# The second long convolution in the first one's step order, and the last slice's two halves in PSUM tiles of their own

## The chip, the cores and the metric

The kernel runs on one core of one Trainium2 chip. The metric is the device time of one execution in microseconds (us); lower is better. Engines are named as the profile names them: PE is TensorE (PEld its weight loads), DVE is VectorE, ACT is ScalarE, POOL is GpSimd, SP is the engine whose queue issues most DMAs. PSUM is the memory that PE writes its results to; DVE and ACT copy them from there to SBUF.

## The reference

Two layers, each a long convolution (an S4 state-space model) and a local dilated attention, each behind a layer norm and added to the running `x` (2048 tokens, 512 channels, bfloat16):

```python
def _A_ref(u, ...):                       # long convolution, per channel d
    P = jnp.exp(logdA[:, :, None] * l[None, None, :])
    K = jnp.einsum("dn,dnl,dn->dl", Cc, P, dB).real
    ...
    Yf = Uf * Kf                          # FFT of length 2 L, product, inverse FFT
    y = irfft2(Yf)[..., :L] + u * Dskip
def _B_ref(x, wqkv, wo):                  # 32 heads of 16, window of 8 keys, dilation 2
    ...
x = A_u
x = x + _A_ref(_layernorm(x), ...)
x = x + _B_ref(_layernorm(x), B_wqkv, B_wo)
x = x + _A_ref(_layernorm(x), ...)
x = x + _B_ref(_layernorm(x), B_wqkv, B_wo)
```

Both convolutions use the same parameters, so the spectrum of `K` is computed once.

## The kernel before

The program first computes the convolution kernel's spectrum (`kgen`), stores it in DRAM (`kt_scratch`), and runs the first stage of the first layer's transform into `Z`. Then for each of the two layers (`layer` 0 and 1) come the rest of the convolution (`a_steps`, `a_layer`), and the attention (`b_layer`), which in layer 0 also writes the first stage for layer 1 into its `Z`.

**One convolution** works on 16 slices (`cg`) of 32 channels. Each slice goes through these steps, named by letters in the dictionary `a.step`:

- `T` (`transposes`, line 254): eight PE transposes of `Z` into the PSUM tile `pt` (pool `psT`, two buffers of one bank).
- `t` or `a` (`transposed`, line 260): `pt` is copied to `zt`, by DVE (`t`) or by ACT (`a`).
- `X` (`second_stage`, line 266): two matmuls of 512 columns into `xp` (pool `psX`, a single buffer of two banks).
- `c` (`second_stage_out`, line 272): ACT copies `xp` to `xc`.
- `p` (`times_spectrum`, line 279): DVE multiplies `xc` with the spectrum `Kt` into `pab`. In layer 1 it also issues the load of the spectrum six slices on (`load_k`, line 236: two DMAs on SP's queue). In layer 0 those loads are words of their own (`k`).
- `v` (`inverse`, line 290): sixteen matmuls into `vp` (two buffers of two banks, which the tiles of y share).
- `V` (`inverse_out`): `vp` is copied to `VT`, by ACT (line 299). For the last slice, number 15, `parts` gives two halves of four groups: `c` and `p` are done in halves, and of `V` ACT does the first half and DVE the second (line 297).

**The order of the steps.** An engine takes its instructions in program order, so the order in which the steps are called sets each engine's queue. In layer 0 it is written out by hand, as the words with `@` at the end of the string `KGEN`. In layer 1 it is a loop in `a_layer`: at turn `cg` it calls `X(cg) c(cg) T(cg+2) t(cg+2) v(cg-2) V(cg-2) p(cg)`. In the steady part of `KGEN` a turn reads like `@X9 @V6 @p8 @k13 @v7 @c9 @t11 @T12`.

**Behind the last slice.** `y_rows` computes the convolution's output from `VT`: matmuls with the transposed first-stage matrix `F1T` (lines 339 and 340) and the residual (line 343) into `ps_y`. The first such tile is done in two column ranges, 0 to 479, which needs slices 0 to 14 only, and 480 to 511, which needs slice 15. The last of four groups also adds a correction from `kU` (line 342), row 0 of a normed tile, which four small DVE operations prepare (lines 328 and 330; in the trace they write `N`). They are put behind `a.last`, so far DVE's copy of the last half. The y steps and all of the attention follow in an order that is written out by hand too (`LAYERS`).

`issue_after(ins)` places what a block issues on the engine of `ins` behind `ins` in that engine's queue.

Of the kernel before, what the change touches and what calls it, by code (L numbers as in the profile page):

```python
# [12 lines left out]
ALU = mybir.AluOpType  # L13
# [203 lines left out]
def a_steps(nc, tc, C, Ng, kt_dram, load_w, layer, Z, es, es_y, psS=None):  # L217
# [10 lines left out]
    def parts(cg):  # L228

        return (slice(0, 4), slice(4, 8)) if cg == NGR // 8 - 1 else (slice(0, 8),)  # L230
# [43 lines left out]
    def times_spectrum(cg):  # L274
        pab, xc, kt = pabp.tile([128, 8, 2, 128], BF, name="pab", tag="pab"), xcs.pop(cg), kts.pop(cg)
        pabs[cg] = pab
        for gs in parts(cg):
            n = gs.stop - gs.start
            nc.vector.tensor_tensor(pab[:, gs], xc[:, gs].to_broadcast([128, n, 2, 128]), kt[:, gs], ALU.mult)  # L279
        if layer and cg + KT_BUFS[layer] < 16:  # L280
            load_k(cg + KT_BUFS[layer])
        if cg == 14 and layer == 0:
            load_w()

    def inverse(cg):
        vp = vps[cg] = a.psS.tile([128, 8, 128], F32, name="vp", tag="psS" if psS is None else "psg")
        pab = pabs.pop(cg)
        for g in range(8):
            for ab in range(2):
                nc.tensor.matmul(vp[:, g, :], pab[:, g, ab, :], C["IC"][:, ab, :], start=(ab == 0), stop=(ab == 1))  # L290

    def inverse_out(cg):
        dst = VT[:].rearrange("k r j d -> k (r j) d")[:, :, cg * 32:(cg + 1) * 32].rearrange("k q (e g) -> k q e g", e=GE)
        src = vps.pop(cg)[:].rearrange("k g (q e) -> k q e g", e=GE)
        for gs in parts(cg):
            if gs.start:
                a.last = nc.vector.tensor_copy(dst[..., gs], src[..., gs])
            else:
                nc.scalar.copy(dst[..., gs], src[..., gs])  # L299

    a.step = dict(T=transposes, t=transposed, a=lambda cg: transposed(cg, True), X=second_stage, c=second_stage_out,
                  p=times_spectrum, v=inverse, V=inverse_out, k=load_k)
    return a


def a_layer(nc, tc, C, Xg, Ng, kt_dram, layer, Z, es_z, a=None):

    if a is None:
        with ExitStack() as es:
            es.enter_context(es_z)  # L310
            a = a_steps(nc, tc, C, Ng, kt_dram, None, layer, Z, es, ExitStack())
            with tc.manual_schedule():
                for cg in range(-2, 18):
                    if 0 <= cg < 16:
                        a.step["X"](cg)
                        a.step["c"](cg)
                    if cg + 2 < 16:
                        a.step["T"](cg + 2)
                        a.step["t"](cg + 2)
                    if cg >= 2:  # L320
                        a.step["v"](cg - 2)
                        a.step["V"](cg - 2)
                    if 0 <= cg < 16:
                        a.step["p"](cg)
    VT, F1T, psS, tag, ident = a.VT, a.F1T, a.psS, "psg" if layer == 0 else "psS", C["ident"]
    kU = Ng[NG - 1]
    with tc.issue_after(a.last.ins):
        nc.vector.tensor_tensor(kU[0:1], Ng[0][0:1], C["klast"][:].unsqueeze(1).to_broadcast([1, 4, D]), ALU.mult)
    for i in range(1, 4):
        nc.vector.tensor_tensor(kU[0:1, i, :], kU[0:1, i - 1, :], kU[0:1, i, :], ALU.add)  # L330
    def y_rows(g, hf):

        ps = psS.tile([128, 2, D], F32, name="ps_y", tag=tag)
        for cols in (slice(0, D - 32), slice(D - 32, D)) if g + hf == 0 else (slice(0, D),):
            for jj in range(2):
                j4 = hf * 2 + jj
                j = g * 4 + j4
                end = cols.stop == D
                nc.tensor.matmul(ps[:, jj, cols], F1T[:, j, 0, :], VT[:, 0, j, cols], start=(cols.start == 0), stop=False)
                nc.tensor.matmul(ps[:, jj, cols], F1T[:, j, 1, :], VT[:, 1, j, cols], start=False, stop=False)  # L340
                if g == NG - 1:
                    nc.tensor.matmul(ps[:, jj, cols], C["last_tok"][:], kU[:, j4, cols], start=False, stop=False)
                nc.tensor.matmul(ps[:, jj, cols], ident[:], Xg[g][:, j4, cols], start=False, stop=end)
        return ps
    return y_rows, a.es_y


# [23 lines left out]
PLUS = (13,)  # L371
WHOLE = (1, 2, 3, 4, 5, 6)
FIRST_LOADS = [("rows_end", 3), ("rows_end", 3), ("stored", 2, 2), ("stored", 3, 2)]
# [3 lines left out]
def kgen(nc, tc, C, prm, kt_dram, Zf, norm_row, norm_rstd, norm_apply, norm_apply_row, norm_tiles, load_rest, es_a, es_y, open_conv):  # L377
    everything = KGEN.split()
    with ExitStack() as es:
# [364 lines left out]
        def conv_step(kind, g):  # L744
            conv[0].step[kind](g)
        for g in range(16):
            for kind, needs in dict(T="", t="T", a="T", X="ta", c="X", p="c", v="p", V="v").items():
                need = [f"@{k}{g}" for k in needs if f"@{k}{g}" in everything]
                if kind == "T":
                    need = ["c2"] + [f"s{c}{i}" for c in range(4) for i in range(2)] + [w for w in everything if w[0] == "z"]  # L750
# [862 lines left out]
```

## Time and profile before

| | us |
|---|---|
| time, median of 3 runs | 438.28 |
| lowest and highest of the 3 | 436.13, 438.46 |
| the profiled execution's own time | 439.68 |
| its span, first to last instruction | 437.9 |

PE is busy for 379.9 us of the span (87%), DVE for 402.4 (92%), ACT for 329.6 (75%), POOL for 25.5 (6%). The mean granted clock of PE is 0.977 of full speed. The two convolutions lie at about 122.8 to 157.4 us and 283.6 to 319.9 us of the span.

In a row of a timeline stand the start, the busy time, the engine and line, the operation, what it writes and reads, shapes and the number of instructions in the row, and in brackets the idle time of the engine before it with what ended it. Rows of several overlapping instructions give the time in which at least one ran.

### The profile page before, as it was taken

How to read it: one execution, taken by the hardware profiler on the slowest of the kernel's cores; microseconds unless marked ns; L12 is line 12 of the kernel's file. 1: busy time of each engine (PE TensorE's matmuls, PEld its weight loads, DVE VectorE, ACT ScalarE, POOL GpSimd, SP SyncE). 2: the span in 40 equal slices, each digit the busy share in tenths (PEclk: the TensorE clock that was granted, in tenths of full speed). 3: DMA queues.
4: the chain of work that ended last, by engine and by line, in shares of the span. 5: the costliest groups of instructions: out<-in, count | busy, mean ns of one | idle time of the engine just before them, and what ended most of it. 6: DMA issues, size and time to landing. Idle time of an engine off the chain costs nothing.

```text
span 437.9 us, 12189 instructions
## 1 busy us (share of the span) xinstructions
PE 379.9 (87%) x5045; PEld 259.3 (59%) x5084; DVE 402.4 (92%) x783; ACT 329.6 (75%) x604; POOL 25.5 (6%) x66
## 2 busy tenths in 40 slices
PE   1176799999989989999997899789899999996995
PEld 1032586676468745686685465367746578784562
DVE  6999989999889969799999999999789999999993
ACT  6999979998989979755665399979969666652442
POOL 5000002001210000020010000000000002020000
PEclk9998779999999999999999899999999999999998
DMA  7900001254889930016043007458100003562022
GB/s 237 419 10 0 1 3 44 74 168 115 250 241 274 297 117 4 1 31 140 3 89 82 0 4 217 168 153 277 57 0 3 1 1 62 110 115 56 1 98 98
DMA packets 25647, 44.06 MB, mean 101 GB/s; under 512 B 7285, under 2 KB 17206, under 8 KB 24950
## 3 DMA queue, kind: packets, MB, share of 16 engines
q1 hardware_dynamic: 22630, 37.30, 29.4%
q0 software_dynamic: 1856, 4.53, 4.4%
q10 hardware_dynamic: 1104, 1.44, 0.9%
q8 instruction: 40, 0.66, 0.7%
q14 instruction: 17, 0.14, 0.1%
HBM read 29.01 MB, written 6.95 MB: 82 GB/s over the span
## 4 chain that ended last, share of the span: by engine, by line
PE 44%; DVE 21%; ACT 21%; issue 7%; DMA 6%; SPq 0%; POOL 0%; DVEq 0%; ACTq 0%; POOLq 0%
PE ps_qk L1170 10%; DVE prodpv L1352 7%; PE ps_v L1257 5%; PE psk L561 4%; DVE prodqk L1220 3%; PE Lp L1242 3%; PE psg L594 3%; ACT xc L272 3%; ACT Z L1426 3%; DVE Z L497 2%; PE pt L254 2%; PE vp L290 2%; PE xp L266 2%; DMA V<-V 2%; ACT X L1406 2%
## 5 line engine op out<-in xcount | busy, mean ns | idle before, releaser
L1352 DVE TENSOR_TENSOR prodpv<-V,Lsb 128x512 bf16<-128x512 bf16 (+1 forms) x124 | 79.4, 701 | 1.2 <-PE po L1362 1.1
L1170 PE MATMUL ps_qk<-xnT,wqk 128*128 128x512 bf16 x256 | 60.3, 379 | 0.0
L1362 PE MATMUL po<-halves,prodpv 128*128 128x64 bf16 x1024 | 38.9, 193 | 7.4 <-DVE prodpv L1352 5.8
L1218 DVE TENSOR_TENSOR prodqk<-qT,N 128x1024 bf16<-128x1024 bf16 (+3 forms) x88 | 42.5, 539 | 2.6 <-ACT N L1173 2.2
L1362 PEld LDWEIGHTS <-prodpv 128*128 128x128 bf16 x1024 | 34.8, 98 | 16.5 <-DVE prodpv L1352 11.1
L279 DVE TENSOR_TENSOR pab<-xc,Kt 128x2048 bf16<-128x2048 bf16 (+1 forms) x34 | 39.2, 1160 | 2.9 <-ACT xc L272 2.8
L1220 DVE TENSOR_TENSOR prodqk<-qT,N 128x512 bf16<-128x512 bf16 (+3 forms) x56 | 40.6, 762 | 0.7 <-ACT N L1173 0.6
L1373 ACT CAST oT<-po 128x512 bf16<-128x512 f32 x32 | 18.3, 595 | 27.4 <-PE po L1362 27.4
L1170 PEld LDWEIGHTS <-wqk 128*128 128x128 bf16 x256 | 23.9, 97 | 23.8
L272 ACT CAST xc<-xp 128x1024 bf16<-128x1024 f32 (+1 forms) x34 | 34.3, 1020 | 4.1 <-PE pt L254 2.8
L299 ACT CAST VT<-vp 128x1024 bf16<-128x1024 f32 (+1 forms) x32 | 33.2, 1052 | 3.1 <-PE vp L290 3.1
L290 PE MATMUL vp<-sb_IC,pab 128*128 128x128 bf16 x512 | 33.8, 219 | 1.2 <-ACT VT L299 0.4
L290 PEld LDWEIGHTS <-pab 128*128 128x128 bf16 x512 | 30.6, 98 | 6.0 <-issue 1.9
L1242 PEld LDWEIGHTS <-prodqk 128*128 128x128 bf16 x1024 | 29.6, 96 | 4.1 <-DVE prodqk L1218 0.6
L1242 PE MATMUL Lp<-sb_bones,prodqk 128*128 128x8 bf16 x1024 | 30.5, 166 | 0.2 <-DVE prodqk L1220 0.2
L1257 PE MATMUL ps_v<-wv,xnT 128*128 128x256 bf16 x256 | 30.4, 272 | 0.0
L521 PE MATMUL psadd<-Z,sb_ident 128*128 128x512 bf16 (+3 forms) x49 | 17.8, 376 | 12.6 <-DVE Z L497 8.2
L1389 PE MATMUL ps_o<-wo_t,oT 128*128 128x512 bf16 x91 | 26.4, 396 | 0.8 <-issue 0.2
L1257 PEld LDWEIGHTS <-xnT 128*128 128x128 bf16 x256 | 24.3, 97 | 3.6
L1173 ACT CAST qT<-ps_qk 128x512 bf16<-128x512 f32 x32 | 18.8, 593 | 7.5 <-PE ps_qk L1170 7.5
L1123 DVE BATCH_NORM_STATS2 ln_stats<-X 128x6 f32<-128x512 bf16 x37 | 23.7, 675 | 0.8 <-ACT X L1447 0.8
L1281 POOL DMA_DIRECT2D V<-V x16 | 8.9, 561 | 255.8 <-ACT V L1264 228.4
(201 smaller groups left out, 854.1 us busy)
## 6 DMA issues: line engine op xcount, KB each, us to landing
Kt<-kt_scratch SPq DMA_DIRECT2D x60, 256.0 KB
kt_scratch<-ks SPq DMA_DIRECT2D x32, 128.0 KB
G<-c_G SPq DMA_DIRECT2D x2, 1536.0 KB
V<-V SPq DMA_DIRECT2D x8, 288.0 KB
X<-in_A_u_dram SPq DMA_DIRECT2D x4, 512.0 KB
F1Tsb<-c_F1T SPq DMA_DIRECT2D x2, 1024.0 KB
V<-V SPq DMA_DIRECT2D x4, 512.0 KB
V<-V POOLq DMA_DIRECT2D x4, 384.0 KB, 7.3
```

The costliest lines, as they stand in the source:

```text
L272: nc.scalar.copy(xc[:, gs].rearrange("q g o l -> q (g o l)"), xp[:].rearrange("q h n -> q (h n)")[:, gs.start * 128:gs.stop * 128])
L279: nc.vector.tensor_tensor(pab[:, gs], xc[:, gs].to_broadcast([128, n, 2, 128]), kt[:, gs], ALU.mult)
L290: nc.tensor.matmul(vp[:, g, :], pab[:, g, ab, :], C["IC"][:, ab, :], start=(ab == 0), stop=(ab == 1))
L299: nc.scalar.copy(dst[..., gs], src[..., gs])
L1170: nc.tensor.matmul(t.ps[:], wqk[:, ct, f0:f0 + 128], x_group(g)[:, :, ct], start=(ct == 0), stop=(ct == 3))
L1218: nc.vector.tensor_tensor(b.pr[:, u:u + 2 * n, 1 - halves_of[0], :], q, cols(kT[i][:, starts[0]:starts[0] + n * 128]), ALU.mult)
L1220: nc.vector.tensor_tensor(b.pr[:, u:u + 2 * n].rearrange("f u a q -> f a u q")[:, ::-1], q.unsqueeze(1).to_broadcast([128, 2, 2 * n, 64]), ...
L1242: nc.tensor.matmul(t.Lp[:, w, u % 2, u // 2, :], b.pr[:, u].rearrange("f a q -> f (a q)"), bones[:], start=False, stop=(t.parts == W // 2 ...
L1257: nc.tensor.matmul(t.ps[:, jj, :], tokens(ct, jp * 2 + jj, c), wv[:, ct, fp * 256:(fp + 1) * 256], start=(jj + ct == 0), stop=(jj == 1 and ...
L1352: nc.vector.tensor_tensor(t.p2[:, c:c + k, 0:nj, :].rearrange("p c j (d h) -> p c j d h", d=DH), m.V2[i // 2][:, c0 + c:c0 + c + k, r0:r0 ...
L1362: nc.tensor.matmul(po[jj // k][:, jj % k, c, :], t.p2[:, c - c0, jj, :], fold, start=(first and c == c0 and jj % k == 0), stop=(last and c ...
L1389: nc.tensor.matmul(t["ps"][:], m.oT[:, ft, j * 128:(j + 1) * 128], wo_t[:, ft, :], start=(added and ft == 0), stop=False)
```

## The change

- Layer 1's convolution runs the words with `@` from `KGEN`, but for the loads (`k`), instead of its loop. Two of the sixteen `zt` copies (`@a1`, `@a3`) are then made by ACT.
- `inverse` and `inverse_out` get a part. Slice 15's two halves are computed into two tiles of their own from the pool `psT`, each of one bank, by `v` and a new step `i`; both are copied to `VT` by ACT, by `V` and a new step `I`. This holds for both layers.
- `a.last`, behind which the four small DVE operations are put, is now DVE's last product `p`.
- The first matmul of y is put behind the last inverse matmul (`a.last_pe`) in PE's queue.

```diff
@@ times_spectrum
-            nc.vector.tensor_tensor(pab[:, gs], xc[:, gs].to_broadcast([128, n, 2, 128]), kt[:, gs], ALU.mult)
+            a.last = nc.vector.tensor_tensor(pab[:, gs], xc[:, gs].to_broadcast([128, n, 2, 128]), kt[:, gs], ALU.mult)
...
-    def inverse(cg):
-        vp = vps[cg] = a.psS.tile([128, 8, 128], F32, name="vp", tag="psS" if psS is None else "psg")
-        pab = pabs.pop(cg)
-        for g in range(8):
+    def inverse(cg, part=0):
+        gs = parts(cg)[part]
+        n = gs.stop - gs.start
+        if n == 8:
+            vp = a.psS.tile([128, 8, 128], F32, name="vp", tag="psS" if psS is None else "psg")
+        else:
+            vp = psT.tile([128, n, 128], F32, name="vp", tag="psT")
+        vps[cg, part] = vp
+        for g in range(n):
             for ab in range(2):
-                nc.tensor.matmul(vp[:, g, :], pab[:, g, ab, :], C["IC"][:, ab, :], start=(ab == 0), stop=(ab == 1))
+                a.last_pe = nc.tensor.matmul(vp[:, g, :], pabs[cg][:, gs.start + g, ab, :], C["IC"][:, ab, :], start=(ab == 0), stop=(ab == 1))
-    def inverse_out(cg):
+    def inverse_out(cg, part=0):
         dst = ...
-        src = vps.pop(cg)[:].rearrange("k g (q e) -> k q e g", e=GE)
-        for gs in parts(cg):
-            if gs.start:
-                a.last = nc.vector.tensor_copy(dst[..., gs], src[..., gs])
-            else:
-                nc.scalar.copy(dst[..., gs], src[..., gs])
+        nc.scalar.copy(dst[..., parts(cg)[part]], vps.pop((cg, part))[:].rearrange("k g (q e) -> k q e g", e=GE))
 
     a.step = dict(T=transposes, t=transposed, a=lambda cg: transposed(cg, True), X=second_stage, c=second_stage_out,
-                  p=times_spectrum, v=inverse, V=inverse_out, k=load_k)
+                  p=times_spectrum, v=inverse, V=inverse_out, i=lambda cg: inverse(cg, 1), I=lambda cg: inverse_out(cg, 1), k=load_k)
@@ a_layer
-                for cg in range(-2, 18):
-                    if 0 <= cg < 16:
-                        a.step["X"](cg)
-                        a.step["c"](cg)
-                    if cg + 2 < 16:
-                        a.step["T"](cg + 2)
-                        a.step["t"](cg + 2)
-                    if cg >= 2:
-                        a.step["v"](cg - 2)
-                        a.step["V"](cg - 2)
-                    if 0 <= cg < 16:
-                        a.step["p"](cg)
+                for word in KGEN.split():
+                    if word[0] == "@" and word[1] != "k":
+                        a.step[word[1]](int(word[2:]))
@@ y_rows
-                nc.tensor.matmul(ps[:, jj, cols], F1T[:, j, 0, :], VT[:, 0, j, cols], start=(cols.start == 0), stop=False)
+                with tc.issue_after(a.last_pe.ins) if g + hf + jj == 0 else nullcontext():
+                    nc.tensor.matmul(ps[:, jj, cols], F1T[:, j, 0, :], VT[:, 0, j, cols], start=(cols.start == 0), stop=False)
@@ KGEN
-        ... @c15 @v14 @V13 @p15 @V14 @v15 @V15")
+        ... @c15 @v14 @V13 @p15 @V14 @v15 @V15 @i15 @I15")
```

More of the change, by code (lines that the diff above doesn't have):

```diff
@@ L746, in kgen @@
         for g in range(16):
-            for kind, needs in dict(T="", t="T", a="T", X="ta", c="X", p="c", v="p", V="v").items():
+            for kind, needs in dict(T="", t="T", a="T", X="ta", c="X", p="c", v="p", V="v", i="v", I="i").items():
                 need = [f"@{k}{g}" for k in needs if f"@{k}{g}" in everything]
```

2 rows, old and new, of the table KGEN are left out of this document.

## The prediction

> **What bounds the kernel now.** I read the page's head and its chain of waits first, then busy time by stage, then the timelines of both convolutions, whose ends the change rewrites.
>
> ```profile
> span 437.9 us, 12189 instructions
> PE 44%; DVE 21%; ACT 21%; issue 7%; DMA 6%; SPq 0%; POOL 0%; DVEq 0%; ACTq 0%; POOLq 0%
> 129.30:152.10 22.80, 21.83 (x303) 18.50 (x305) 21.96 (x25) 22.80 (x26) 0.00 (x0) 1.00 0.99 279
> 157.40:190.00 32.60, 32.47 (x279) 19.64 (x281) 29.27 (x75) 25.99 (x49) 0.00 (x0) 1.00 0.01 4
> 290.40:314.70 24.30, 22.48 (x307) 18.84 (x311) 21.87 (x24) 23.37 (x26) 0.00 (x0) 1.00 0.68 205
> 319.90:350.00 30.10, 29.93 (x262) 16.76 (x264) 29.09 (x79) 23.53 (x39) 0.00 (x0) 1.00 0.01 2
> ```
>
> The first two lines are the page's, the other four are stages: stretch, length, then busy us (and instructions) of PE, weight loads, DVE, ACT, POOL, the granted clock, DMA share, GB/s. The whole-kernel chain names no one engine, so the stages decide. In the first convolution (second of the four) ACT is busy all 22.80 us. In the second one it is busy 23.37 of 24.30: it waits. After each convolution PE is busy 32.47 of 32.60 and 29.93 of 30.10: whatever lets y start earlier moves all that follows by as much.
>
> **Part 1, the second convolution's steps.** First convolution, then second:
>
> ```profile
> 122.80 1.07 PE L254 MATMUL pt<-sb_ident,Z 128*128 128x128 bf16 x16 [0.23 <-DVE Z L634]
> 123.95 1.01 ACT L260 COPY zt<-pt 128x1024 bf16<-128x1024 bf16 x1 [0.23 <-PE pt L254]
> 124.89 1.01 ACT L272 CAST xc<-xp 128x1024 bf16<-128x1024 f32 x1
> 130.21 1.06 ACT L272 CAST xc<-xp 128x1024 bf16<-128x1024 f32 x1
> 152.11 1.22 ACT L272 CAST xc<-xp 128x512 bf16<-128x512 f32 x2
> ```
>
> ```profile
> 283.63 1.07 PE L254 MATMUL pt<-sb_ident,Z 128*128 128x128 bf16 x16 [0.68 <-ACT Z L1426]
> 285.66 1.01 ACT L272 CAST xc<-xp 128x1024 bf16<-128x1024 f32 x1 [2.09 <-PE pt L254]
> 291.30 1.02 ACT L272 CAST xc<-xp 128x1024 bf16<-128x1024 f32 x1
> 308.92 1.02 ACT L272 CAST xc<-xp 128x1024 bf16<-128x1024 f32 x1
> 310.12 1.01 ACT L299 CAST VT<-vp 128x1024 bf16<-128x1024 f32 x1 [0.19 <-PE vp L290]
> 314.67 1.11 ACT L272 CAST xc<-xp 128x512 bf16<-128x512 f32 x2
> ```
>
> Both work 16 slices with the same operations. Slice 3's xc copy starts at 130.21 and 291.30, slice 15's at 152.11 and 314.67: 21.90 us against 23.37 for 12 slices, 1.825 us a slice against 1.948. In the second convolution a VT copy waits 0.19 us for PE ("PE vp"); xc to VT is then 1.20 us (308.92 to 310.12). The cause is in the order: the loop puts X and T of later slices ahead of v(cg-2) in PE's queue, and X waits for the single xp buffer, so v is late. The first one's order puts v directly behind X. With it I take the first one's pace: 23.37 - 21.90 = 1.47 us. Its prologue, from the first transposes to slice 3's xc copy, is 130.21 - 122.80 = 7.41 us against 291.30 - 283.63 = 7.67: 0.26 more. Sum 1.73 us.
>
> The new order moves two zt copies from DVE to ACT (slices 1 and 3). Slice 1's runs in the first convolution at 123.95, ahead of xc, and xc still starts 2.09 us after the transposes (124.89 - 122.80) against 2.03 in the second; it fits where ACT now waits 2.09 us for PE. The 7.41 us contain slice 3's too. If that cover failed, one copy's pitch, 124.89 - 123.95 = 0.94 us, would be lost. So this term lies between 0.8 and 1.8 (the upper end with a slice 0.01 shorter still); I take 1.73, since the order, shapes and buffers are those of the measured convolution.
>
> PE and DMA must carry the pace. PE: 21.83 busy of 22.80 at just this pace, full clock. The spectrum loads (L236) are issued on SP inside p, six slices ahead; their order on SP stays, only their times move.
>
> ```profile
> Kt<-kt_scratch SPq DMA_DIRECT2D x60, 256.0 KB
> DMA to landing us min/median/max: 5.5/5.9/6.4
> 139.00:145.00 6.00, 5.54 (x78) 4.69 (x78) 5.98 (x7) 6.00 (x8) 0.00 (x0) 1.00 1.04 290
> 296.00:302.00 6.00, 5.53 (x79) 4.66 (x79) 5.42 (x7) 5.81 (x7) 0.00 (x0) 1.00 0.87 280
> ```
>
> The first row is from the page's DMA issues, the second ends the answer on the tile Kt. Two loads of 256 KB a slice in 1.825 us are 287 GB/s; the first convolution moved 290 at a DMA share of 1.04, the second now 280 at 0.87. So the engines would be full, but the lead is 6 x 1.825 = 10.95 us against 5.9 to land: 5 us of cover. At 280 GB/s a slice's data take 1.87 us, and ten loads slip by under 0.5 us. Cost nothing; with the cover gone the pace would be 1.87, and 12 x 0.05 = 0.6 us of the gain be lost.
>
> [...]
>
> **Part 2, the last slice, in both layers.**
>
> ```profile
> 151.70 2.10 PEld L290 LDWEIGHTS <-pab 128*128 128x128 bf16 x33
> 151.91 1.96 PE L290 MATMUL vp<-sb_IC,pab 128*128 128x128 bf16 x32
> 152.95 1.29 DVE L279 TENSOR_TENSOR pab<-xc,Kt 128x1024 bf16<-128x1024 bf16 x2 [0.21 <-ACT xc L272]
> 153.07 2.09 ACT L299 CAST VT<-vp 128x1024 bf16<-128x1024 f32 x2
> 154.30 0.61 PE L290 MATMUL vp<-sb_IC,pab 128*128 128x128 bf16 x8 [0.43 <-DVE pab L279]
> 155.21 0.36 PE L339 MATMUL ps_y<-VT,F1Tsb 128*128 128x480 bf16 x1 [0.31 <-ACT VT L299]
> 155.41 0.61 PE L290 MATMUL vp<-sb_IC,pab 128*128 128x128 bf16 x8
> 155.86 0.37 PE L340 MATMUL ps_y<-VT,F1Tsb 128*128 128x480 bf16 x1
> 156.06 0.58 ACT L299 CAST VT<-vp 128x512 bf16<-128x512 f32 x1 [0.90 <-PE vp L290]
> 156.67 0.37 PE L343 MATMUL ps_y<-X,sb_ident 128*128 128x480 bf16 x1
> 156.68 0.69 DVE L297 CAST VT<-vp 128x512 bf16<-128x512 f32 x1 [2.43 <-ACT VT L299]
> 157.28 1.20 DVE L328 TENSOR_TENSOR N<-N,klast 1x2048 bf16<-1x2048 bf16 x1
> 157.42 0.18 PE L339 MATMUL ps_y<-VT,F1Tsb 128*128 128x32 bf16 x1 [0.39 <-DVE VT L297]
> 317.67 0.36 PE L339 MATMUL ps_y<-VT,F1Tsb 128*128 128x480 bf16 x1 [0.31 <-ACT VT L299]
> 319.87 0.18 PE L339 MATMUL ps_y<-VT,F1Tsb 128*128 128x32 bf16 x1 [0.39 <-DVE VT L297]
> ```
>
> y's first tile does columns 0 to 479 (six matmuls) as soon as slice 14 lies in VT, and the last 32 when slice 15 does. Now: y's first matmul goes at 155.21, between the halves of slice 15's inverse; the second half runs at 155.41; only then ACT copies half one (156.06), only then DVE half two (156.68), and the 32 columns start at 157.42.
>
> After: 33 weight loads by 153.80 show that slice 15's first weights were ready; its matmuls at 154.30 waited although PE ended slice 14's at 151.91 + 1.96 = 153.87. Slice 13's buffer, which ACT frees a copy's pitch before 155.16 (below), so near 154.25, came just then; a tile of its own takes that out. The eight start at 153.87, the other eight behind them, both products being done at 152.95 + 1.29 = 154.24. A group's own 0.61 us each puts their end at or before 155.1. ACT is done with slice 14 at 153.07 + 2.09 = 155.16, then copies two halves of 0.58: 156.32, without any overlap. Y's first matmul still starts at 155.21, being bound by slice 14's copy, so standing behind the last inverse costs it nothing. Its six matmuls, undivided, at (156.67 - 155.86) / 4 = 0.2025 us each end their issue at 155.21 + 1.215 = 156.43. The halves are in by then: the 32 columns start at 156.43 instead of 157.42, a gain of 0.99. In the second layer 317.67 + 1.215 = 318.89 against 319.87: 0.98. What is late next is PE itself. If a half on ACT took DVE's 0.69, VT would be full at 156.54 and 0.11 a layer be lost.
>
> Four DVE operations on N (L328, then three of L330) move ahead of y into DVE's idle 2.43 us; only y's last group reads them. If that cover were gone they would stand where they stand now. DVE has then 2.4 us less beside y's first rows; PE is the bound there, so at most PE's remaining gap of 0.17 us (30.10 - 29.93) is gained. The psT buffers of transposes 14 and 15 were freed slices earlier: nothing.
>
> **Sum.** 1.73 + 0.99 + 0.98 = 3.70 us off a span of 437.9: 434.2. The profiled execution took 439.68, 1.78 more than its span; it would take 435.98. The three runs' median is 438.28, 1.40 below that execution, so I predict 434.6.
>
> **The rivals.** *Y waits for more than slice 14.* If the new queue place, or copies that are all on one engine, make y's first matmul wait for both halves, it starts near 156.37, its six take to 157.58, and each tail loses 0.16. Left: 1.73 - 0.32 = 1.4, time 436.9. Against it: y's matmul at 155.21 did not wait for the half copied at 156.06. For it: the very queue order is changed.
>
> *The order does not bring the pace.* If the second convolution stays at 1.948 us a slice for a reason of its own, only the tails are left: 1.97 us, 436.3. Against it: its waits are named, and its operations last no longer (1.02 against 1.06 for xc).
>
> *Slower: the granted clock falls.* The change makes PE's work in the second convolution denser and lets another 30 us of dense work follow.
>
> ```profile
> 43.80:54.70 10.90, 7.67 (x126) 6.10 (x126) 10.90 (x17) 10.71 (x25) 0.32 (x1) 0.76 0.01 2
> 240.80:251.80 11.00, 9.61 (x101) 5.36 (x102) 9.93 (x23) 4.12 (x11) 0.00 (x0) 0.84 0.00 0
> ```
>
> The clock was 0.84 and 0.76 there. PE needs 21.83 / 22.80 x 1.825 = 1.75 us a slice; below a clock of 0.90 that exceeds 1.948 and the step order turns into a loss. At 0.84 it is 2.08 us: 12 slices take 25.0, 3.1 more than forecast, and the 29.93 us behind it 5.7 more. Net 3.7 - 8.8 = 5.1 us slower, 443.4. Against it: the four dense stages all have 1.00, and both low clocks lie where PE was less busy (7.67 of 10.90, 9.61 of 11).
>
> [...]
>
> *The gain is given back later*, at a transfer or an engine that is not late now: up to 3 us, 437.6. PE's 32.6 and 30.1 us without gaps leave little room.
>
> **How the numbers follow.** Forecast 0.72, y's wait 0.08, no pace 0.10, clock 0.06, given back 0.04. A measurement of this kernel can tell about 0.5% (2.2 us) from no change: faster is below 436.1. Nearly all of the forecast's cases are; the second, third and fifth cases are not. So faster 0.72, same 0.22, slower 0.06. The forecast's ends: 0.8 instead of 1.73 in part 1 and 0.2 less in the tails give 435.7; 0.3 more gain, and runs that go as far below the median as the lowest of the three (436.13, 2.15 less), give 432.2. The range reaches up to 436.9 to take in the third case and the second: 432.2 to 436.9.
>
> **What would show it.** Right: in the second convolution slice 3 to slice 15 takes about 21.9 us with no VT copy behind "PE vp"; both half copies on ACT directly behind slice 14's; the 128x32 matmuls directly behind six 128x480 without idle time; L328 before them; clock 1.00. Wrong: slice 15's xc copy more than 30 us behind the first transposes (152.11 - 122.80 = 29.3 forecast, 31.0 now), y's first matmul behind the last half copy, DVE's products waiting for Kt, or a PE gap between y and the projections.

## The result, and the profile after

The changed kernel took 433.23 us, the median of nine runs (431.72 to 435.78). The kernel before, in nine runs beside them, took 438.46 (436.13 to 439.73). The ratio is 0.9902 with a 95% interval from 0.9880 to 0.9924: the kernel became faster by 4.3 us (3.3 to 5.3). (The ratio rests on all eighteen runs; the two medians alone lie 5.2 us apart.) The forecast was 434.6, a ratio of 0.9916. The profiled execution took 432.04 us, its span 430.1.

The page's head and its chain of waits:

```profile
span 430.1 us, 12189 instructions
...
PE 47%; DVE 21%; ACT 18%; DMA 6%; issue 6%; SPq 0%; POOL 0%; DVEq 0%; ACTq 0%
```

ACT's share of the chain fell from 21% to 18%, PE's rose from 44% to 47%. Stages come next: first convolution, what follows it, second convolution, what follows that (the columns are those of the first fence of the prediction).

```profile
127.80:150.60 22.80, 21.83 (x302) 18.50 (x305) 21.95 (x25) 22.80 (x27) 0.00 (x0) 1.00 1.00 283
154.90:187.50 32.60, 32.49 (x280) 19.64 (x281) 27.51 (x72) 25.99 (x49) 0.00 (x0) 1.00 0.02 6
285.80:308.70 22.90, 21.88 (x304) 18.60 (x307) 21.85 (x24) 22.90 (x27) 0.00 (x0) 1.00 0.75 225
313.00:343.00 30.00, 29.89 (x263) 16.83 (x264) 27.65 (x76) 23.72 (x40) 0.00 (x0) 1.00 0.01 2
```

The third row is the one to compare: ACT is now busy all 22.90 us of the second convolution, as in the first one, where it had been busy 23.37 of 24.30. The clock is 1.00 in all four. The timeline of the second convolution shows the same:

```profile
279.42 1.07 PE L254 MATMUL pt<-sb_ident,Z 128*128 128x128 bf16 x16 [0.68 <-ACT Z L1418]
280.52 1.01 ACT L260 COPY zt<-pt 128x1024 bf16<-128x1024 bf16 x1 [1.16 <-PE pt L254]
281.45 1.01 ACT L272 CAST xc<-xp 128x1024 bf16<-128x1024 f32 x1
286.76 1.06 ACT L272 CAST xc<-xp 128x1024 bf16<-128x1024 f32 x1
308.67 1.22 ACT L272 CAST xc<-xp 128x512 bf16<-128x512 f32 x2
```

Slice 3's xc copy starts at 286.76, slice 15's at 308.67: 21.91 us where it had been 23.37. From the first transposes to slice 3's xc copy it is 7.34 us, where it had been 7.67. Now the tails, layer 0 and then layer 1:

```profile
151.54 3.07 ACT L299 CAST VT<-vp 128x1024 bf16<-128x1024 f32 x4
152.55 1.21 DVE L319 TENSOR_TENSOR N<-N,klast 1x2048 bf16<-1x2048 bf16 x1
153.68 0.36 PE L331 MATMUL ps_y<-VT,F1Tsb 128*128 128x480 bf16 x1 [0.37 <-ACT VT L299]
154.69 0.37 PE L335 MATMUL ps_y<-X,sb_ident 128*128 128x480 bf16 x1
154.89 0.18 PE L331 MATMUL ps_y<-VT,F1Tsb 128*128 128x32 bf16 x1
...
311.77 0.36 PE L331 MATMUL ps_y<-VT,F1Tsb 128*128 128x480 bf16 x1 [0.37 <-ACT VT L299]
312.98 0.18 PE L331 MATMUL ps_y<-VT,F1Tsb 128*128 128x32 bf16 x1
```

The four copies on ACT are one run without gaps. The six 128x480 matmuls go from 153.68 to 154.89 undivided, and the 128x32 ones stand directly behind them: 1.21 us in both layers instead of 2.21 and 2.20.

Where the 7.8 us between the two spans (437.9 and 430.1) lie, cut at the first transposes of each convolution and at its first 128x32 matmul:

| stretch | before | after | difference |
|---|---|---|---|
| start to first transposes (nothing changed there) | 122.80 | 121.26 | -1.54 |
| first convolution | 34.62 | 33.63 | -0.99 |
| from it to the second one (first attention) | 126.21 | 124.53 | -1.68 |
| second convolution | 36.24 | 33.56 | -2.68 |
| from it to the end (second attention) | 118.03 | 117.12 | -0.91 |

The second and fourth rows are what the forecast spoke of: 3.67 of 3.70 us. In the last row 0.23 us belong to the change too (below). The first row is not the change's: in the profiles that follow, that stretch was anything from 121.2 to 123.9 us, with the same code. What the third row and the rest of the last one are is the matter of the last experiments and of the account behind them.

### The profile page after: what moved, and what is told of

It is laid out like the page before. It is cut to its first block, busy times and chain, and to the rows that moved or that the text cites. A ratio compares the mean times of both kernels' runs of the same rounds, so it can differ in the third digit from the quotient of the medians.

```text
span 430.1 us, 12189 instructions
## 1 busy us (share of the span) xinstructions
PE 377.7 (88%) x5045; PEld 260.6 (61%) x5084; DVE 400.3 (93%) x779; ACT 331.4 (77%) x608; POOL 25.3 (6%) x66
## 4 chain that ended last, share of the span: by engine, by line
PE 47%; DVE 21%; ACT 18%; DMA 6%; issue 6%; SPq 0%; POOL 0%; DVEq 0%; ACTq 0%
PE ps_qk L1162 10%; PE psk L553 6%; DVE prodpv L1344 6%; PE ps_v L1249 5%; DVE prodqk L1212 3%; PE Lp L1234 3%; DVE Z L489 3%; ACT Z L1418 3%; PE psg L586 3%; PE po L1354 2%; DMA V<-V 2%; DMA Kt<-kt_scratch 2%; ACT X L1398 2%; ACT xc L272 2%; PE ps_y L335 2%
## 5 line engine op out<-in xcount | busy, mean ns | idle before, releaser
L1354 PE MATMUL po<-halves,prodpv 128*128 128x64 bf16 x1024 | 41.3, 198 | 5.6 <-DVE prodpv L1344 4.4
L1354 PEld LDWEIGHTS <-prodpv 128*128 128x128 bf16 x1024 | 37.1, 101 | 14.6 <-DVE prodpv L1344 8.9
L272 ACT CAST xc<-xp 128x1024 bf16<-128x1024 f32 (+1 forms) x34 | 35.8, 1067 | 1.4 <-PE pt L254 0.7
L299 ACT CAST VT<-vp 128x1024 bf16<-128x1024 f32 (+1 forms) x34 | 35.7, 1101 | 0.0
L513 PE MATMUL psadd<-Z,sb_ident 128*128 128x512 bf16 (+3 forms) x49 | 16.7, 353 | 12.9 <-DVE Z L489 8.2
L1381 PE MATMUL ps_o<-wo_t,oT 128*128 128x512 bf16 x91 | 25.1, 379 | 0.6
```

Of the source, the lines that this page charges most:

```text
L272: nc.scalar.copy(xc[:, gs].rearrange("q g o l -> q (g o l)"), xp[:].rearrange("q h n -> q (h n)")[:, gs.start * 128:gs.stop * 128])
L299: nc.scalar.copy(dst[..., parts(cg)[part]], vps.pop((cg, part))[:].rearrange("k g (q e) -> k q e g", e=GE))
L1354: nc.tensor.matmul(po[jj // k][:, jj % k, c, :], t.p2[:, c - c0, jj, :], fold, start=(first and c == c0 and jj % k == 0), stop=(last and c ...
```

## The experiments

All stretches below are cut as above and come from one profile each; the times "before" are those of the kernel before, run beside the experiment. In the code, `...` marks what is left out.

**1. The order alone.** The kernel before, with the loop of layer 1 replaced by the words of `KGEN`; tails as they were.

```diff
-                for cg in range(-2, 18):
-                    ...
+                for word in KGEN.split():
+                    if word[0] == "@" and word[1] != "k":
+                        a.step[word[1]](int(word[2:]))
```

> Theory (the step order and the two tails are separate terms that add): only the second convolution changes. From slice 3's xc copy to slice 15's it takes about 21.9 us (before 23.37), no VT copy waits for PE, and its tail is the old one: y's 32 columns start 2.2 us behind its first matmul in both layers. Time 1.7 us below before. Rival (the order only pays together with the new tail, or not at all): 23.4 us for the 12 slices, time as before.

Measured: 436.43 us (12 runs) against 438.02 (31 runs) before, ratio 0.9953 (0.9929 to 0.9978). Timeline of the second convolution, slices 3 and 15:

```profile
290.89 1.05 ACT L272 CAST xc<-xp 128x1024 bf16<-128x1024 f32 x1
312.79 1.22 ACT L272 CAST xc<-xp 128x512 bf16<-128x512 f32 x2
```

21.90 us for 12 slices; the convolution took 34.55 instead of 36.24, 1.69 us less, with the old tail of 2.21 in both layers. Part 1 stands alone, as forecast (1.73).

**2. The tails alone.** The changed kernel with the old loop, and slice 15's second half called at its end.

```diff
                     if cg >= 2:
                         a.step["v"](cg - 2)
                         a.step["V"](cg - 2)
+                    if cg == 17:
+                        a.step["i"](15)
+                        a.step["I"](15)
```

> Theory: the second convolution keeps its old pace (23.4 us for 12 slices, VT copies waiting 0.19 us for PE), but in both layers the 32 columns start 1.2 us behind y's first matmul, so 1.0 us earlier each; with the gap of 0.2 us that PE has between the second layer's y and its projections gone too. Time 2.0 to 2.2 us below before. Rival: the tails pay nothing of their own (y is bound by slice 14 anyhow), time as before.

Measured: 435.19 us (8 runs) against 438.02, ratio 0.9937 (0.9914 to 0.9960). Timeline, layer 1: slices 3 and 15, then y's first tile.

```profile
288.91 1.02 ACT L272 CAST xc<-xp 128x1024 bf16<-128x1024 f32 x1
312.28 1.10 ACT L272 CAST xc<-xp 128x512 bf16<-128x512 f32 x2
...
315.27 0.36 PE L343 MATMUL ps_y<-VT,F1Tsb 128*128 128x480 bf16 x1 [0.37 <-ACT VT L299]
316.48 0.18 PE L343 MATMUL ps_y<-VT,F1Tsb 128*128 128x32 bf16 x1
```

The old pace (23.37) with the new tail (1.21): the convolutions took 33.63 and 35.24, 0.99 and 1.00 less. The two parts do not touch each other: 1.69 and 1.99 us of the convolutions, together 3.68, against 3.67 in the whole change. (The runs, 0.47% and 0.63% against 0.98%, are too coarse to show that: each is known to about 0.25%.)

**3. What in the order matters.** The kernel before, with one block of its loop moved: `v` and `V` ahead of `T` and `t`. Nothing of `KGEN`, no copy moved to ACT.

```diff
                         a.step["X"](cg)
                         a.step["c"](cg)
-                    if cg + 2 < 16:
-                        a.step["T"](cg + 2)
-                        a.step["t"](cg + 2)
                     if cg >= 2:
                         a.step["v"](cg - 2)
                         a.step["V"](cg - 2)
+                    if cg + 2 < 16:
+                        a.step["T"](cg + 2)
+                        a.step["t"](cg + 2)
```

> The kernel before with one edit: in the loop of the second convolution v and V are called ahead of T and t. Theory A (the pace was lost because T stood ahead of v in PE's queue): 12 slices take 22 us or a little more, no VT copy waits for PE, time 1.0 to 1.5 us below before. Rival B (it is the smaller lag, the prologue or the zt copies on ACT in the hand-written order that set the pace): 23.4 us as before, same time.

Measured: 436.74 us (12 runs) against 438.02, ratio 0.9959 (0.9938 to 0.9980). ACT's waits in the second convolution up to slice 15's xc copy, before:

```profile
engine line waited for: us in total, times, longest us
ACT xc L272 <- PE pt L254: 2.1, 1, 2.1
ACT xc L272 <- PE xp L266: 1.4, 2, 0.7
ACT VT L299 <- PE vp L290: 1.3, 6, 0.3
```

and in this kernel:

```profile
ACT xc L272 <- PE xp L266: 3.4, 3, 2.1
```

The waits at the start are the same 3.4 and 3.5 us (those for `pt` and `xp` in the prologue); the row of six VT copies that waited 1.3 us for PE's `vp` is gone. The 12 slices take 21.87 us and the convolution 34.41, 1.83 less than before and 0.14 less than with the words of `KGEN`. So the prediction's cause holds in a narrower form: the inverse of slice cg-2 stood behind the transposes of slice cg+2 in PE's queue, and that cost 0.12 us a slice. `X(cg)`, which the prediction named beside them, stands ahead of that inverse here too, and no VT copy waits.

**4. The queue edit alone taken out.** The changed kernel without `issue_after` on y's first matmul.

```diff
-                with tc.issue_after(a.last_pe.ins) if g + hf + jj == 0 else nullcontext():
+                if True:
```

> The changed kernel without the edge that queues y behind the last inverse matmul; three of y's matmuls then stand ahead of all of slice 15's inverse in PE's queue. Theory: y's first matmul waits for slice 14's copy and holds slice 15's inverse behind it, so both half copies start over 1 us later and the 32 columns start about 2.3 us behind y's first matmul instead of 1.2: 1.0 to 1.2 us lost in each layer, 2.0 to 2.4 us in all against the changed kernel. Rival (the edge changes nothing, the own tiles do it all): 1.2 us as in the changed kernel, same time as it.

Measured: 436.09 us (12 runs) against 438.02, ratio 0.9950 (0.9926 to 0.9975): of the change's 4.3 us, 2.2 are left by the ratio. Timeline, layer 0:

```profile
154.64 0.36 PE L331 MATMUL ps_y<-VT,F1Tsb 128*128 128x480 bf16 x1 [1.10 <-ACT VT L299]
155.25 1.06 PE L295 MATMUL vp<-sb_IC,pab 128*128 128x128 bf16 x16
155.90 1.07 ACT L299 CAST VT<-vp 128x512 bf16<-128x512 f32 x2 [1.30 <-PE vp L295]
157.02 0.18 PE L331 MATMUL ps_y<-VT,F1Tsb 128*128 128x32 bf16 x1
```

This is what the edit prevents. y's first matmul stands ahead of slice 15's inverse and waits for slice 14's copy; the whole inverse, whose operands are ready, waits behind it; ACT then idles 1.30 us. The tail is 2.38 us (2.37 in layer 1), longer than the 2.21 before. The second convolution is 1.16 us longer than in the changed kernel. The first is 1.66 longer; the 0.50 beyond that go with a wait of DVE for a late Kt load (0.6 us), not with the queue.

**5. The second half on DVE again**, its tile its own.

```diff
-        nc.scalar.copy(dst[..., parts(cg)[part]], ...)
+        (nc.vector.tensor_copy if part else nc.scalar.copy)(dst[..., parts(cg)[part]], ...)
```

> The changed kernel, but DVE copies slice 15's second half again, out of its own tile. Theory: the old wait of DVE for ACT came from the shared tile, or from the interleaved writes to VT; either way VT is full before PE has done y's six matmuls, so the 32 columns start 1.2 us behind y's first matmul as in the changed kernel: it does not matter which engine makes the second copy. If the tile was the cause, DVE's copy overlaps ACT's. Rival (both copies on ACT are what earns the 1.0 us): 1.5 to 2.2 us.

One run: 432.95 us; tails 1.21 and 1.21, stretches 33.63 and 33.56, as in the changed kernel. Timeline, layer 1:

```profile
310.59 2.58 ACT L299 CAST VT<-vp 128x1024 bf16<-128x1024 f32 x3
312.74 0.67 DVE L299 CAST VT<-vp 128x512 bf16<-128x512 f32 x1
```

DVE starts its half at 312.74, while ACT copies the other one until 310.59 + 2.58 = 313.17. Before, with the halves in two banks of one tile, DVE's copy started at 156.68, directly behind ACT's (156.06 + 0.58 = 156.64), though its matmuls were done at 155.41 + 0.61 = 156.02: of the 2.43 us for which DVE stood idle, the last 0.66 were a wait for ACT. So that wait came with the one tile: out of two tiles the copies ran side by side for 0.43 us (312.74 to 313.17). Which engine copies the second half makes no difference to the tails and stretches.

**6. One tile for both halves**, both copied by ACT, both inverses ahead of both copies.

```diff
...
+        if part:
+            vp = vps[cg, 0]
...
-        "... @v14 @V13 @p15 @V14 @v15 @V15 @i15 @I15")
+        "... @v14 @V13 @p15 @V14 @v15 @i15 @V15 @I15")
```

> The changed kernel, but both halves of slice 15 in one tile of the old pool (slice 13's buffer), sixteen matmuls and then two copies by ACT. The prediction's working: the inverse starts when ACT frees slice 13's buffer, about 0.5 us later than with tiles of its own, and the first copy waits for all sixteen matmuls; VT is full at or just behind the sixth y matmul. So 1.2 to 1.4 us from y's first matmul to the 32 columns: the own tiles are worth 0.2 us a layer at most. Rival (the own tiles are the core of the gain): 1.8 us or more.

One run: 433.29 us. Timeline, layer 0:

```profile
153.84 1.05 PE L295 MATMUL vp<-sb_IC,pab 128*128 128x128 bf16 x16 [0.43 <-DVE pab L279]
154.75 0.36 PE L331 MATMUL ps_y<-VT,F1Tsb 128*128 128x480 bf16 x1
154.93 1.07 ACT L299 CAST VT<-vp 128x512 bf16<-128x512 f32 x2 [0.22 <-PE vp L295]
156.05 0.18 PE L331 MATMUL ps_y<-VT,F1Tsb 128*128 128x32 bf16 x1
```

The inverse waits 0.43 us again, as before the change, since it needs slice 13's buffer. (The bracket names DVE's product, which was done at about the same time. In layer 1 the same wait, of this kernel at 312.01 and of the kernel before at 316.75, is put down to "ACT VT", the copy of slice 13.) y's first tile takes 1.30 us instead of 1.21, the convolution 33.71 instead of 33.63. The tiles of their own, one of the three edits of part 2, are worth 0.09 us a layer; the place of y in the queue is worth most of the 0.99. A kernel with that place alone, one tile and the old copy on DVE, was not run.

**7. All zt copies on DVE** in the second convolution.

```diff
-                        a.step[word[1]](int(word[2:]))
+                        a.step[word[1].replace("a", "t")](int(word[2:]))
```

> The changed kernel with the second convolution's two zt copies that moved to ACT back on DVE. Theory: they were hidden where ACT waited for PE: from the first transposes to slice 3's xc copy 7.3 us in both, within 0.2. Rival (they cost their pitch on ACT): 0.9 us less here than in the changed kernel.

One run: 433.0 us; the second convolution took 33.42 us instead of 33.56. The two copies moved to ACT cost 0.14 us of the 1.88 that two copies take (2 x 0.94): not quite nothing, but nearly hidden. Experiments 1 and 3, with and without those two copies on ACT, differ by the same 0.14.

**8. More filler in the first attention.** In the trace before, a stretch of it ran at half clock (last section). This kernel is the changed one with at least 768 columns of filler matmuls ahead of each group of the attention's value products.

```diff
+                    if not last_layer and j0 == 0 and i > 0:
+                        plan.fill = max(plan.fill, 768)
                     stream(po[0][:], first)
```

> The changed kernel with 768 columns of zero matmuls put ahead of each of twelve groups of po matmuls in the first attention, where PE is busy only half of the time. Theory (the attention behind the first convolution lasts 124.5 us in the changed kernel's profile and 125.8 to 126.5 in four others because a spell of half clock of 3.4 us or twice that begins at a different point in each, 80 to 87 us behind y's 32 columns): with PE busier ahead of it the spell is gone, and the stage takes 124.0 to 124.6 us in any run; the median falls by 0 to 1.5 us, and the runs lie closer together. Rival (the stage is shorter because of the change itself, the clock has no part): the stage stays at 124.5 with the spell still there, or gets longer by the added matmuls.

Measured: 433.54 us (6 runs, 432.53 to 434.20), ratio 0.9904 (0.9881 to 0.9928). The profile has no spell, but neither have those of experiments 5, 6, 7 and 12, which have no filler, so one profile does not show that the filler removed it. The stretch took 125.14 us, neither the 124.0 to 124.6 expected nor less than the changed kernel's 124.53: the filler costs 0.6 us of its own. The six runs lie within 1.67 us (3.46 in six runs of the changed kernel, experiment 11), as expected, but their median is no lower. Missed in the main. (The first convolution took 34.54 us here, 0.91 more than in the changed kernel, with its last two products late; the edit lies behind it.)

**9. The four operations on N behind the half copy**, with that copy on DVE.

```diff
+        copied = (nc.vector.tensor_copy if part else nc.scalar.copy)(dst[..., parts(cg)[part]], ...)
+        a.last = copied if part else a.last
```

> The changed kernel with slice 15's second half on DVE and the four operations on N back behind that copy: of the tail only the own tiles and the queue place are left. Theory: 1.2 us from y's first matmul to the 32 columns stays; from there to the first transposes behind the second layer's y it takes 8.75 us as in the kernel before, against 8.52 in the changed one: the four operations are worth 0.2 us in the second layer and nothing in the first. Rival (they bear no part): 8.5 us.

(The times of 8.75 and 8.52 us in that text are to a later point of the same chain; to the first `pt_x` transposes they are 328.45 - 319.87 = 8.58 and 321.33 - 312.98 = 8.35.) One run: 434.51 us. y to the transposes took 8.36 us, so the theory that the place behind the copy costs 0.2 fell. What does cost it is not tested by an edit of its own, but can be read from ACT's timeline in layer 1, of the kernel before:

```profile
324.11 1.01 ACT L1447 CAST X<-ps_y 128x1024 bf16<-128x1024 f32 x1 [0.28 <-PE ps_y L343]
325.48 0.30 ACT L1129 ACTIVATE ln_den<-ln_mv,eps 128x4 f32<-128x4 f32 x1 [0.36 <-DVE ln_mv L1126]
325.68 0.99 ACT L1447 CAST X<-ps_y 128x1024 bf16<-128x1024 f32 x1
```

of the changed kernel:

```profile
317.22 1.01 ACT L1439 CAST X<-ps_y 128x1024 bf16<-128x1024 f32 x1 [0.28 <-PE ps_y L335]
318.13 0.30 ACT L1121 ACTIVATE ln_den<-ln_mv,eps 128x4 f32<-128x4 f32 x1
318.51 1.01 ACT L1439 CAST X<-ps_y 128x1024 bf16<-128x1024 f32 x1
```

and of this kernel, on DVE and ACT:

```profile
314.08 0.69 DVE L299 CAST VT<-vp 128x512 bf16<-128x512 f32 x1 [0.72 <-PE vp L295]
314.69 1.20 DVE L320 TENSOR_TENSOR N<-N,klast 1x2048 bf16<-1x2048 bf16 x1
...
320.85 0.30 ACT L1122 ACTIVATE ln_den<-ln_mv,eps 128x4 f32<-128x4 f32 x1
321.15 1.01 ACT L1440 CAST X<-ps_y 128x1024 bf16<-128x1024 f32 x1
```

The operations on N delay DVE's layer norm (before, three of them of 0.4 us each lie between its first steps, from 320.98 to 323.25; after, they are done at 311.88 + 1.30 = 313.18, ahead of its first step at 314.37), for which ACT waits (0.36 us, before) ahead of a copy out of `ps_y`, and PE waits for that buffer: before, the copy ends at 325.68 + 0.99 = 326.67, and PE's next matmul starts at 326.73, 0.45 us behind the one ahead of it (326.28); after, the copy ends at 318.51 + 1.01 = 319.52, and that step is 0.22 (319.39 to 319.61). Counted from the 128x32 matmuls, that copy starts at 325.68 - 319.87 = 5.81 us before and at 318.51 - 312.98 = 5.53 after; here, too, it is 5.53. In this kernel DVE's half copy no longer waits for ACT, so N starts 0.9 us ahead of the 128x32 matmuls instead of 0.1. As far as these rows show, what counts is the lead: the earlier place in the queue (changed kernel) and a copy that does not wait (this one) both give it.

**10 and 11. Slice 14 in halves as well, beside the changed kernel again.** Slice 14's halves go to two tiles of `psT`, one copied by ACT and one by DVE, slice 15's to one tile, both by ACT; all zt copies are on DVE. Number 11 is the changed kernel as it is, on the same chip.

```diff
...
-        "... @v14 @V13 @p15 @V14 @v15 @V15 @i15 @I15")
+        "... @v14 @i14 @V13 @p15 @V14 @I14 @v15 @i15 @V15 @I15")
```

> A version meant to beat both kernels: slice 14's two halves get the tiles of their own and are copied by ACT and DVE side by side, slice 15 goes into one tile of the old pool with both copies on ACT, and the second convolution's zt copies are on DVE. Theory (y is bound by slice 14's copy, and two engines can copy from two tiles at once): y's first matmul comes 0.3 to 0.4 us earlier in both layers, and the second convolution's start is 0.14 us shorter: 33.2 to 33.3 us for the first convolution from its first transposes to the 32 columns (33.63 in the changed kernel), 33.0 to 33.1 for the second (33.56); 0.8 to 0.9 us in all, hardly to be told in the times. Rival (the second copy waits for the first in any case, or slice 15 becomes late in its place): no gain, or 0.3 us lost in each tail.

> The changed kernel once more, beside the version above on the same chip: 33.6 us for each convolution, 124.5 us for the attention between them if no spell of half clock falls into its dense part and up to 2 us more if one does; time 4 to 5 us below before.

Measured: 433.23 us (6 runs), ratio 0.9891 (0.9855 to 0.9927), against 433.78 for the changed kernel (6 runs), 0.9886 (0.9855 to 0.9917): no difference that these runs can tell. In number 11 the convolutions took 33.63 and 33.56 us and the attention 124.54, as expected. In number 10 the second convolution took 33.12 us, 0.44 less: 0.14 by experiment 7's edit and 0.30 because y's first matmul came earlier (2.80 us behind slice 15's xc copy, against 3.10), as expected. The first took 34.79, because its last slices came late. DVE's waits there:

```profile
DVE pab L279 <- ACT VT L305: 0.9, 1, 0.9
DVE zt L260 <- PE pt L254: 0.8, 1, 0.8
DVE pab L279 <- DMA Kt<-kt_scratch: 0.5, 1, 0.5
```

Experiment 4, which lacks this edit, has the first and the third of these waits as well (0.9 and 0.6 us), so the edit is not shown to cause them. Its gain is shown in the second convolution alone; the times do not show one over the changed kernel.

**12. A delay on purpose.** Five matmuls of 512 columns of zeros ahead of y's second tile in layer 0, to bring the first attention about 1 us later and see whether the spell of half clock in it moves.

```diff
+        for _ in range(5 if layer == 0 and (g, hf) == (0, 1) else 0):
+            nc.tensor.matmul(ps[:, 0, :], ident[:], C["zero"][:].to_broadcast([128, D]), start=True, stop=True)
```

> The changed kernel with five zero matmuls of 512 columns (1.08 us of PE) ahead of y's second tile in the first layer, so that all behind the first convolution comes as late as with the old tail. In the profiles so far the attention behind it takes 124.5 us wherever the first convolution lasts 33.6 to 33.7 us, and 125.8 to 126.5 wherever it lasts 34.6 or more; the half-clock spell lies elsewhere in it. Theory (the point at which the spell falls depends on when that attention comes, so a shift of 1 us brings more than 1 us): the stage, with the 1.08 us in it, takes 126.9 to 127.6 us, and the median rises by 2 to 3 us over the changed kernel's 433.2 to 433.8. Rival (chance): 125.6 us, and a median up by 1.1 us.

Measured: 433.64 us (10 runs, 432.76 to 435.44), ratio 0.9921 (0.9892 to 0.9950). The first attention's stretch took 125.62 us, 1.09 more than the changed kernel's 124.53, about what five matmuls of 512 columns take by themselves (from 155.60 to the next matmul at 156.69 it is 1.09); there was no spell. The first convolution took 34.08 us, 0.45 more than in the changed kernel, with DVE waiting 1.0 us for Kt loads ahead of the edit, so the attention came about 1.5 us later and not 1.1. The median is no 2 to 3 us higher either. The theory, that 1 us of shift brings the spell back into the dense part, fell.

## Why the prediction was right

*The order's pace.* Right in size, 1.47 us forecast and 1.46 measured (23.37 to 21.91), and in cause but for one point: experiment 3 gave the whole term by moving one block of the loop, so it was the transposes between X and v that made v late; X stands ahead of v there as well and waits for ACT's copy of its single buffer three times, 1.7 us in all (nine times and 2.8 us before), without making a VT copy wait ahead of slice 15. The prologue gave 0.33 instead of 0.26; from slice 15's xc copy to y's first matmul it is 0.10 longer (3.00 us before, 3.10 after). Experiment 1 gave 1.69 for the forecast sum of 1.73.

*The zt copies at no cost.* Nearly: 0.14 us (experiment 7) of the 0.94 a copy that their cover was worth. The forecast took the first convolution's pace with such copies in it, so the sum was not touched.

*The Kt loads at no cost.* Right for the second convolution: ACT is busy all the time at DMA share 0.75 (0.92 and 272 GB/s from 291.3 to 297.3 us), and DVE waits for no Kt there.

*The copies' pitch.* The 12 slices of two copies each took 21.91 / 24 = 0.913 us a copy in the second convolution; in the first one before it was 21.90 / 24 = 0.9125.

*The tails.* 0.99 and 0.98 forecast, 0.99 and 1.00 measured alone (experiment 2). y's first matmul waits for slice 14's copy only, as forecast, and the half copies hide behind six matmuls. Here one reason was put in a wrong light. The prediction led with the tile of its own that "takes that out", the wait for slice 13's buffer, and counted the queue edit as costing nothing. Experiments 4 and 6 turn that round: the wait was as the prediction read it, but the tile that removes it is worth 0.09 us, and without the queue edit the tail is 2.38 us, longer than before. Both halves' inverse matmuls ahead of y is what gives the gain. The forecast end of the tail was right all the same, since y's six matmuls set it and not the copies.

*The operations on N.* "At most PE's remaining gap of 0.17 us" was a bound that was too low: the gap worth gaining was 0.23 (8.58 to 8.35 us from y to the transposes), and it was gained in every kernel with the new tail. It was left out of the sum.

*The sum.* 3.70 us forecast. By the trace the change's own terms are 0.99 + 2.68 + 0.23 = 3.90. The runs say 4.3, with an interval from 3.3 to 5.3 that holds both. So the 7.8 us between the two profiled spans are not all the change's: 1.54 lie where nothing changed, and 1.68 in the first attention. Those 1.68 are a spell of half clock, told in the last section: profiles without a spell (but for experiments 8 and 12, which add matmuls there), and those with an early one, show 124.5 us from y to the second convolution, with old and new step order alike; late spells give 125.8 to 126.5. What the change has to do with it is open. The three profiled kernels with the old tail all had late ones (126.21, 126.48, 126.11), but so had two with the new tail (125.79, 126.05). All five had a first convolution of 34.6 us or more, and the seven with 33.6 to 33.7 show 124.5; but experiment 12's shift did not bring a late spell. Whether the change makes it rarer is not shown.

The other 0.68 us of the table's last row do not lie in the attention. From the `pt_x` transposes to the end of the last computing instruction, ACT's copy out of `ps_o`, it is 104.99 us before and 105.00 after; from there to the end of the span, where the last outputs are stored, it is 4.46 before and 3.77 after. Of the other profiles experiment 3 has 4.42 there and all the rest 3.76 to 3.80, experiment 1 with its old tail among them, so it did not come with the tails. Its cause is open.

*The rivals.* None happened. y does not wait for both halves (0.37 us of idle time ahead of it, ended by slice 14's copy); the order brought the pace; the clock stayed 1.00 in the dense stages, though the work became denser, as the row of the third stage shows. Nothing behind gave the gain back: no stretch of the table is longer than before.

## What to carry to other kernels

When an engine waits a little in every turn of a loop (0.12 us a turn here, six longer waits in the view), look at what stands ahead of its supplier in the supplier's queue; moving one block of the loop was worth 1.8 us, as much as a whole order written by hand. In experiment 4 an instruction that waited held up all that stood behind it in its queue (PE stood idle for 1.10 us ahead of y, with slice 15's inverse behind y, and ACT then for 1.30 us): put the one that waits longest (y, for slice 14's copy) behind the ones whose operands are ready (slice 15's inverse), and check by taking out that one edit, since it may carry the gain that a more visible edit seems to bring. A difference of two profiled spans holds chance as well (7.8 us against the 4.3 of the runs); cut it at marks that the change can't move before explaining it.

## What the hardware showed that was not expected

In nine of the fourteen profiles the granted clock drops to half (0.50 in the rows) for about 3.4 or 6.8 us in the first attention, at a place that moves. Stretches of the kernel before:

```profile
237.80:241.20 3.40, 2.08 (x49) 1.59 (x49) 3.40 (x5) 0.13 (x1) 0.00 (x0) 1.00 0.02 5
...
244.40:247.40 3.00, 2.85 (x7) 1.06 (x7) 3.00 (x5) 0.55 (x1) 0.00 (x0) 0.50 0.00 0
```

of the changed kernel:

```profile
233.30:236.70 3.40, 1.34 (x38) 1.10 (x35) 3.40 (x5) 1.52 (x4) 0.00 (x0) 0.97 0.02 5
236.90:239.90 3.00, 2.86 (x46) 2.44 (x44) 3.00 (x6) 0.26 (x1) 0.00 (x0) 0.50 0.00 0
```

and of experiment 5:

```profile
239.00:242.00 3.00, 1.92 (x49) 1.58 (x45) 3.00 (x9) 1.07 (x2) 0.00 (x0) 1.00 0.00 0
242.60:246.00 3.40, 3.35 (x19) 1.53 (x17) 3.40 (x6) 0.81 (x2) 0.00 (x0) 1.00 0.00 0
```

Experiment 5 had no spell, so its rows show what PE needs at full clock. Counted from y's first 128x32 matmul, PE is busy for half to two thirds of the time from 80 to 85 us, for nearly nine tenths to 87, and all the time from there to 94; DVE is busy throughout. In the other two, PE is busy for only 39% to 61% of the 3.40 us stretches of the first part. After, the half clock lies from 236.5 to 239.9, 81.6 to 85.0 us on that count, where PE has time to spare. Before, it lies from 244.1 to 247.5, 86.7 to 90.1 us on that count, where in experiment 5 (its second row) PE has none: half the clock for 3.4 us would lose 1.7 there (an estimate, 3.4 x 0.50), and the stretch is 1.68 longer. The four spells that began at 80.4 to 81.6 us and lasted 3.4 cost nothing (124.52 to 124.54 us, as without a spell); the four of 6.8 us began at 82.1 to 83.0, reached into the dense part and cost 1.3 to 1.9 (125.79 to 126.48 us).

What sets a spell off, and what sets its length and its place, is not shown. In the 3.40 us up to 236.7, in which the spell after began at 236.5, PE was busy for 39% of the time, and the clock was 0.97.

The first convolution's spectrum loads come only just in time (283 GB/s at a DMA share of 1.00 in the changed kernel). In experiments 3, 4, 10 and 12 its last products waited 0.5 to 1.0 us for them, and 0.3 in experiment 6, without any edit of the loads; in the changed kernel they did not. In experiment 12 all that differs from the changed kernel lies behind the convolution, so such a wait can come by chance. The 5 us of cover that the prediction found for the second convolution are not there in the first.
